# Attention and a token-mixing MLP on one core: exponentials over a bank pair, and ScalarE's side work ordered by deadlines

## The chip, the core and the metric

The kernel runs on one core of one Trainium2 chip. A core has TensorE (matmuls, shown in the profile as PE, its weight loads as PEld), VectorE (DVE), ScalarE (ACT), GpSimd (POOL) and SyncE (SP), which here only issues DMAs. Each engine works through its own instructions in order and waits for others at semaphores. Matmuls write to PSUM, eight banks of 512 fp32 columns on each of 128 partitions. The metric is the device time of one execution in microseconds (us).

## What is computed

`x` has 2048 tokens of 640 channels. The output mixes an attention block and a token-mixing MLP by a gate; all of it is fp32.

```
g = sigmoid((x * gate_w).sum(-1))
# A: 32 heads of 20
q, k, v = split(x @ wqkv)
p = softmax(q @ k.T * 20**-0.5)
a = concat(p @ v) @ wo
# B: MLP over the token axis, shared by the channels
h = layernorm(x)                       # over the 640 channels
u = gelu(einsum("sd,sf->df", h, w1) + b1)   # f = 1728
b = (u @ w2 + b2).T
out = g * a + (1 - g) * b
```

## The kernel before

Precision is kept by splitting each fp32 operand into a high part and a remainder (`hi_lo`, line 38): ScalarE copies the high part, and VectorE or GpSimd subtracts it from the source. A product is then three matmuls (high by high, high by low, low by high).

The program is one stream of Python calls. Engines whose order is "manual" (`manual_schedule`) keep the order in which the code emits their instructions: TensorE always, ScalarE and VectorE from the first unit on, GpSimd and SP from the MLP's preparation on. Where an instruction stands in the emission is therefore where it stands in its engine's queue.

The stages, in order of time:

- **Projections.** `qk_unit(m, w, q)` makes 128 rows of q or k for 512 tokens: 15 matmuls into one of four PSUM banks (`st_tile`, tags st0 to st3), then ScalarE copies the high part (`evh`), VectorE makes the remainder (`evl`), and SP stores both. For three row blocks of k it also makes differences of neighbouring blocks (`kf`, `dh`). `load_w` fetches a weight block by a DMA on ScalarE's queue and splits it. After 16 units come 32 units for v, whose weights are `wv`, loaded raw as `wvr` by SP and split by `split_wv`; then 24 more q and k units.
- **MLP, with the first half of the row maxima beside it.** `mlp` is a generator; each step is a pair of matmuls on the two row halves of the array (`pair64`), which run at the same time. It goes through two halves of the channels (`d`); in each, 14 tiles of u and 16 tiles of y. A tile uses two `st` banks. At its end ScalarE evacuates both (`u_evac`: `xg` and `x2`; `y_evac`: `ty` and `x2`), GpSimd adds them; for u follow the gelu and a split into `gh` and `gl`, for y the store to `y_d`. The weights come 512 columns at a time: SP loads `wr` (8 buffers), `w_split` makes `wh` on ScalarE and `wl` on GpSimd, and `w_need(k)` keeps splits four pieces ahead.
- Between MLP steps, `s_next` gives matmuls of a second stream: scores of queries by keys, of which only the row maximum is wanted, so that the exponentials can be shifted. They go in pairs over four banks (s twice, s3, pv). Of eight such matmuls, three (`s_over`) are read by ScalarE (`relu`, line 212, into `ov`), three (`s_two`) by VectorE together with an `ov`, two (`s_one`, line 203) by VectorE alone. 1082 of the 2050 positions of this stream are given beside the MLP.
- **The loop.** 16 pairs of heads, 32 iterations each: 512 iterations. An iteration has four score matmuls with keys on the partitions (`st_op`, line 787), each read by one exponential of 512 columns on ScalarE (line 789), two `s_next` while they last, and the four products p by v of the iteration before (`pv_flush`, line 743), which accumulate in the bank pv. The four scores go round five banks: st0 to st3 and s3.
- **The output.** Normalisation, the product with `wo` (lines 843 to 847) and the mix.

In the MLP, ScalarE's and GpSimd's later steps are held back by a count of MLP steps, and emitted in the loop over steps by `settle`:

```
soon.append([2, relu])                  # s_over: two steps after its matmul
soon.append([6, lambda: ...tensor_add(xg, xg, x2)])
soon.append([18 if f == f_order[-1] else 30, lambda: u_gelu(...)])
while len(w_got) < min(k + 4, len(w_list)):
    w_split(len(w_got))                 # in w_need: at once
```

Of the kernel before, what the change touches and what calls it, by code (L numbers as in the profile page):

```python
# [13 lines left out]
P = 128  # L14
# [16 lines left out]
def gated_mix(ctx, tc, xT, x, wqk, wv0, wv1, wo, w1, w1t, b1, w2, b2, out):  # L31
# [37 lines left out]
    psum = ctx.enter_context(tc.tile_pool(name="psum", bufs=1, space=PSUM))  # L69

    def st_tile(shape, name):
        n = st_count[0] % 4
        st_count[0] += 1
        return psum.tile(shape, F32, tag=f"st{n}", bufs=1, name=name)
# [131 lines left out]
    def s_over(p, half, t, j, kc, over):  # L206
        def f():
            ps = s_mm(p, half, t, j, kc)

            def relu():  # L210
                over[j, kc] = s_pool[0].tile([P, 512], F32, tag="over", bufs=3, name=f"ov{p}_{half}_{t}_{j}_{kc}")
                nc.scalar.activation(over[j, kc], ps, AF.Relu)  # L212
# [81 lines left out]
    def qk_unit(m, w, q):  # L294
# [23 lines left out]
        dh = p1.tile([P, 512], F32R, tag="evh", bufs=2, name=f"dh{c}_{q}")  # L318
# [21 lines left out]
    raws = [w_dma(0), w_dma(NC)]  # L340
    w = {0: load_w(0, raws[0])}
    load_x(0)
    w[NC] = load_w(NC, raws[1])
# [116 lines left out]
    w_raws, w_got = [], []  # L460
# [13 lines left out]
    def w_split(k):  # L474
        src, tail = w_list[k]
        raw = w_raws[k]
        n, m = src.shape[1], src.shape[2]
        if k < AHEAD:
            o = 8 * (k % 2)
            hi, lo = w_tmp[k // 2][:, o: o + 4], w_tmp[k // 2][:, o + 4: o + 8]  # L480
        else:
            hi = gp.tile([P, 4, P], F32R, tag="wh", bufs=5, name=f"wh{k}")
            lo = None if tail else gp.tile([P, 4, P], F32R, tag="wl", bufs=5, name=f"wl{k}")
        if tail:
            hi_lo(hi[:, :n, :m], hi[:, :n, m:], raw[:, :n, :m], hi_eng=nc.scalar, lo_eng=nc.gpsimd)
        else:
            hi_lo(hi[:, :n], lo[:, :n], raw[:, :n], hi_eng=nc.scalar, lo_eng=nc.gpsimd)
        w_got.append((hi, lo))
# [9 lines left out]
    hs = []  # L498
    for n, (m, q) in enumerate(units):
# [4 lines left out]
        if 3 <= n < NT + 3:  # L504
            hs.append(h_split(0, n - 3))
# [26 lines left out]
    soon = []  # L532

    def settle(all_=False):
        for e in soon:
            e[0] -= 1
        due = [e for e in soon if all_ or e[0] <= 0]
        for e in due:
            soon.remove(e)
            e[1]()  # L540

    def u_evac(f, d, ps, gh, gl):
        xg = gp.tile([P, HALF], F32, tag="xg", bufs=3, name=f"xg{d}_{f}")
        nc.scalar.activation(xg, ps[0], AF.Copy)
        x2 = half_sum(ps[1], 1.0)
        soon.append([6, lambda: nc.gpsimd.tensor_add(xg, xg, x2)])
        if f == FF:
            soon.append([7, lambda: u_swap(d, xg)])
            soon.append([70, lambda: nc.gpsimd.tensor_add(xg, xg, sws.pop())])
            soon.append([100, lambda: u_tail(f, d, xg, gh)])  # L550
        else:
            soon.append([18 if f == f_order[-1] else 30, lambda: u_gelu(f, xg, gh, gl)])
# [5 lines left out]

    sws = []

    def u_gelu(f, xg, gh, gl):
        nc.scalar.activation(xg, xg, AF.Gelu_apprx_tanh, bias=b1_t[:, f:f + 1])
        hi_lo(gh, gl, xg, hi_eng=nc.scalar, lo_eng=nc.gpsimd)
# [7 lines left out]
    def u_tail(f, d, xg, gh):  # L571
        nc.scalar.activation(xg, xg, AF.Gelu_apprx_tanh, bias=b1_t[:, f:f + 1])
        ht = gp.tile([P, HALF], F32R, tag="ht", bufs=1, name=f"ht{d}")
        nc.gpsimd.tensor_copy(ht[TL:], xg[TL:])
        nc.gpsimd.tensor_copy(gh[:TL], xg[:TL])
        nc.gpsimd.tensor_sub(gh[TL:], xg[TL:], ht[TL:].bitcast(F32))

    def y_evac(t, d, ps):
        ty = hp.tile([P, HALF], F32, tag="ty", bufs=3, name=f"ty{d}_{t}")
        c = slice(t, t + 1)  # L580
        nc.scalar.activation(ty, ps[0], AF.Identity, bias=b2o[:, c], scale=omg[:, c])
        x2 = half_sum(ps[1], omg[:, c])

        def rest():
            nc.gpsimd.tensor_add(ty, ty, x2)

        def store():
            (nc.sync if d and t == NT - 1 else nc.scalar).dma_start(y_d[t * P:(t + 1) * P, d * HALF:(d + 1) * HALF], ty)

        soon.append([6, rest])  # L590
        soon.append([24, store])

    def mlp(hs):
        k = 0
        for d in range(2):
            g = {}
            for f in f_order:
# [3 lines left out]
                ps = [st_tile([P, HALF], f"u{d}_{f}_{i}") for i in range(2)]  # L601
                for c in range(4):
                    wh, wl = w_need(k)
                    k += 1
                    for i in range(4):
                        hh, hl = hs[4 * c + i]
# [6 lines left out]
                u_evac(f, d, ps, gh, gl)  # L613
                g[f] = (gh, gl)
            for t in range(NT):
                ps = [st_tile([P, HALF], f"y{d}_{t}_{i}") for i in range(2)]
                for c in range(4):
                    wh, wl = w_need(k)
                    k += 1
                    for i in range(4 if c < 3 else 2):  # L620
                        f = 4 * c + i
                        gh, gl = g[f]
# [9 lines left out]
                if d and t == NT - 2:  # L632
                    nc.scalar.activation(eps_t, eps_t, AF.Exp)
                if d == 0:
                    if t == 0:
                        h_norm(1, 0)
                    if t + 1 < NT:
                        h_norm(1, t + 1)
                    hs[t] = h_split(1, t)
                    if t + 3 < NT:  # L640
                        h_load(1, t + 3)
# [11 lines left out]
    for n, _ in enumerate(steps):  # L653
        settle()
# [13 lines left out]
    settle(True)  # L668
# [23 lines left out]
    s_wide[0] = False  # L692
    s_src[NDIFF + 1] = s_stack(NDIFF + 1)
# [85 lines left out]
    def st_op(i):  # L779
        g, n = divmod(i, 4)  # L780
# [3 lines left out]
        j, c = 1 - n % 2, n // 2  # L784
        r = slice(64 * j, 64 * j + 3 * DH + 2)
        ps = psum.tile([P, 512], F32, tag="s3" if i % 5 == 4 else f"st{i % 5}", bufs=1, name=f"st{p}_{it}_{j}{c}")
        nc.tensor.matmul(ps, ks[r, kt * P:(kt + 1) * P], qs[qh][r, c * 512:(c + 1) * 512], start=True, stop=True)  # L787
        pt = lp.tile([P, 512], F32, tag="pt", bufs=12, name=f"p{p}_{it}_{j}{c}")
        nc.scalar.activation(pt, ps, AF.Exp, scale=SCALE)  # L789
        pts.setdefault(g, {})[j, c] = pt  # L790

    st_op(0)
    LEFT = NP * 128 + 2 - S_AHEAD
    for p in range(NP):
# [3 lines left out]
        for it in range(32):  # L798
# [34 lines left out]
    lps.close()  # L833

# [74 lines left out]
```

## Time and profile before

| | us |
|---|---|
| median of 3 runs (1860.96 to 1864.75) | 1861.8 |
| profiled execution, its own time | 1860.5 |
| its span in the profile | 1858.7 |
| projections (first qk matmul to last) | 7.3 to 229.0 |
| MLP with row maxima | 229.3 to 768.9 |
| loop (first exponential to the end of the last) | 770.8 to 1774.5 |
| output | 1775.5 to 1858.7 |

The profiled execution is the one that all rows below are from; it is 1.3 us under the median of the runs. In the rows, a group is "line engine operation, output<-input xcount | busy us, mean ns of one | idle us just before, and what ended it". Busy time counts overlapping instructions once, so a mean of one may be longer than busy time divided by the count: instructions of one engine overlap their start with the end of the one ahead. The table of windows gives, for each stretch, each engine's busy us and in brackets its instructions. A matmul's end is modelled, so TensorE reads as busy even where it has small gaps; its weight loads show those better.

### The profile page before, as it was taken

Reading aid. Unit: us, or ns where it says so; the run is one execution under the profiler, and the core shown is the slowest. Engines: PE = TensorE matmul, PEld = TensorE weight load, DVE = VectorE, ACT = ScalarE, POOL = GpSimd, SP = SyncE. Lnnn points to the kernel's source line nnn. Section 1 sums busy time; section 2 is a strip of 40 time slices with the busy share of each in tenths; the row PEclk is TensorE's granted clock in tenths of the full one; section 3 lists DMA queues with packets and bytes.
Section 4 is the critical chain, followed back from the end, with each engine's and each line's share of the span. In section 5 each row is a group of like instructions: output and inputs, shape, how many; then the busy total and the mean of one; then the engine's idle time right before and its main releaser. Section 6 shows DMA issues by size and latency. Waiting matters only on the chain. (4 is left out here: it accounts for less than half of the span.)

```text
span 1858.7 us, 39442 instructions
## 1 busy us (share of the span) xinstructions
PE 1829.8 (98%) x14978; PEld 1188.1 (64%) x14978; DVE 1239.4 (67%) x2407; ACT 1511.7 (81%) x3047; POOL 640.8 (34%) x898
## 2 busy tenths in 40 slices
PE   9899999999999999999999999999999999999998
PEld 7798799999999999644444444444444444444378
DVE  5303288888888888866666666666766667667137
ACT  4244378877788777599999999999999999999920
POOL 2112367778777777201111211121322121212210
PEclk9999999999999999999999999999999999999999
DMA  8646876556665555225222232042262322201463
GB/s 301 203 152 234 260 184 171 145 158 191 179 179 145 145 155 165 68 55 134 57 48 59 60 85 56 22 109 59 54 124 63 76 62 56 71 14 23 129 217 131
DMA packets 155662, 222.93 MB, mean 120 GB/s; under 512 B 65998, under 2 KB 92382, under 8 KB 152046
## 3 DMA queue, kind: packets, MB, share of 16 engines
q1 hardware_dynamic: 131008, 181.70, 35.8%
q0 software_dynamic: 15104, 23.01, 5.3%
q10 hardware_dynamic: 9360, 15.70, 2.5%
q8 instruction: 118, 1.93, 0.4%
q14 instruction: 72, 0.59, 0.1%
HBM read 165.43 MB, written 54.54 MB: 118 GB/s over the span
## 5 line engine op out<-in xcount | busy, mean ns | idle before, releaser
L203 DVE TENSOR_REDUCE mx<-s 128x1 f32<-128x512 f32 x1280 | 833.1, 686 | 303.0 <-PE s L197 296.6
L789 ACT ACTIVATE p<-st 128x512 f32<-128x512 f32 x2048 | 1003.6, 940 | 0.6 <-PE st L787 0.6
L787 PEld LDWEIGHTS st<-qs_True,ks_True 62*128 62x128 f32 x2048 | 336.0, 185 | 462.6 <-ACT p L789 434.7
L743 PE MATMUL pv<-p,v 128*32 128x512 f32 x4096 | 546.6, 605 | 0.2 <-PE st L787 0.2
L787 PE MATMUL st<-qs_True,ks_True 62*128 62x512 f32 x2048 | 529.3, 437 | 1.1 <-ACT x L556 1.1
L197 PE MATMUL s<-ks_False,qs_False 60*128 60x512 f32 x1152 | 315.2, 407 | 9.7 <-ACT ov L212 8.4
L197 PE MATMUL s<-sk,sq 60*128 60x512 f32 x896 | 324.0, 444 | 0.0
L43 POOL TENSOR_TENSOR wl<-wr,wh 128x512 fp32r<-128x512 f32 x228 | 276.3, 1217 | 107.9 <-ACT wh L40 70.9
L221 DVE CUSTOM_DVE_ANT_0 ov<-s,ov 128x512 f32<-128x512 f32 x384 | 263.6, 687 | 57.5 <-PE s L197 51.3
L212 ACT ACTIVATE ov<-s 128x512 f32<-128x512 f32 x384 | 224.7, 598 | 80.2 <-PE s L197 77.8
L730 POOL DMA_DIRECT2D o_d<-oev x128 | 66.8, 522 | 622.1 <-DVE oev L724 619.5
L48 PE MATMUL y<-gh,wh 64*128 64x320 f32 x896 | 196.7, 307 | 0.0
L48 PE MATMUL y<-gl,wh 64*128 64x320 f32 x832 | 188.3, 307 | 0.0
L48 PE MATMUL y<-gh,wl 64*128 64x320 f32 x832 | 186.5, 306 | 0.0
L40 ACT ACTIVATE wh<-wr 128x512 fp32r<-128x512 f32 (+2 forms) x246 | 147.6, 601 | 46.3 <-DMA wr<-in_wqk_dram 30.7
L197 PEld LDWEIGHTS s<-ks_False,qs_False 60*128 60x128 f32 x1152 | 164.6, 185 | 24.0 <-ACT ov L212 15.4
L743 PEld LDWEIGHTS pv<-p,v 128*32 128x32 f32 x4096 | 81.2, 108 | 125.1 <-issue 115.6
L48 PE MATMUL u<-hl,wh 64*128 64x320 f32 x864 | 161.0, 307 | 0.0
L48 PE MATMUL u<-hh,wh 64*128 64x320 f32 x864 | 160.7, 307 | 0.0
L48 PE MATMUL u<-hh,wl 64*128 64x320 f32 x800 | 149.9, 307 | 0.0
L48 PEld LDWEIGHTS y<-gh,wh 64*128 64x128 f32 x896 | 137.8, 185 | 1.2
L197 PEld LDWEIGHTS s<-sk,sq 60*128 60x128 f32 x896 | 130.7, 184 | 0.0
(129 smaller groups left out, 2108.2 us busy)
## 6 DMA issues: line engine op xcount, KB each, us to landing
wr<-in_w_dram SPq DMA_DIRECT2D x192, 256.0 KB
ks_True<-k_d SPq DMA_DIRECT2D x96, 160.0 KB
qs_True<-q_d SPq DMA_DIRECT2D x192, 80.0 KB
qs_False<-q_d SPq DMA_DIRECT2D x108, 80.0 KB
sk<-k_d SPq DMA_DIRECT2D x42, 160.0 KB
sq<-q_d SPq DMA_DIRECT2D x84, 80.0 KB
v_d<-vt SPq DMA_DIRECT2D x32, 168.0 KB
v<-v_d SPq DMA_DIRECT2D x16, 336.0 KB
```

The costliest lines, as they stand in the source:

```text
L40: nc.scalar.activation(hi, src, AF.Copy)
L43: (lo_eng or nc.vector).tensor_sub(lo, src, hi.bitcast(F32))
L48: nc.tensor.matmul(ps[k], a[r], b[r], start=start, stop=stop)
L197: nc.tensor.matmul(ps, qs[half][r, t * P:(t + 1) * P], ks[r, kc * 512:(kc + 1) * 512], start=True, stop=True)
L203: nc.vector.tensor_reduce(mx[:, slot, j, t: t + 1], ps, axis=AX.X, op=OP.max)
L212: nc.scalar.activation(over[j, kc], ps, AF.Relu)
L221: nc.vector.tensor_tensor_reduce(ov, ps, ov, 1.0, -3.0e38, OP.add, OP.max, mx[:, slot, j, t: t + 1])
L730: nc.gpsimd.dma_start(o_d[DH * h: DH * h + DH, cols], ev[r: r + DH, :])
L743: nc.tensor.matmul(pv[r: r + 32, :], v_tiles[p][:, kt, 10 * j: 10 * j + 32], pt[j, c], start=(kt == 0), stop=(kt == NT - 1))
L787: nc.tensor.matmul(ps, ks[r, kt * P:(kt + 1) * P], qs[qh][r, c * 512:(c + 1) * 512], start=True, stop=True)
L789: nc.scalar.activation(pt, ps, AF.Exp, scale=SCALE)
```

## The change

There are four edits.

**1. The loop's exponentials.** `st_op` is replaced by `st_pair` and `st_one`. In each iteration the two scores of the first 512 queries (heads j = 0 and 1) go to the two banks of one tile `two`, and one exponential of 1024 columns reads both. The other two scores go to single banks (one0, one1 and s3 in turn), each with an exponential of 512 columns. The pair has one buffer: 2 + 2 + 1 + 2 (s) + 1 (pv) are all eight banks. To make room, the four `st` banks get a pool of their own, closed before the loop (`four`), and one is opened again for the output (`late`). The order of TensorE's work changes: pair, one, two maxima, one, products. The score that was given one ahead of the loop is no longer there.

**2. ScalarE's order beside the MLP.** `settle` now takes nanoseconds: a clock advances by 146 for an MLP step and by 233 for a pair of maxima. ScalarE's work is put into a list with a cost, a delay before it may start and a slack (`act`), and whenever ScalarE is free by that clock, the entry that is allowed and has the earliest deadline is emitted. `force` emits from the lists until a condition holds, where something is needed at once. The two evacuations of a tile are separate entries; weight splits, five pieces ahead instead of four, have deadlines too; other steps go into a list of events by time. The stores of y move from ScalarE's queue to SP's.

**3. Loads of weights for the first projections.** The DMAs for the third and fourth weight blocks are issued one or several units earlier, and `wv` is split one unit earlier and ahead of the unit.

**4. The tile `dh`** of the first two k blocks has a buffer of its own instead of one of the two of `evh`.

```
-            soon.append([2, relu])
+            act(relu, 480, 350, 900)
...
+            force(lambda: (j, kc - 1) in over)
...
-        dh = p1.tile([P, 512], F32R, tag="evh", bufs=2, name=f"dh{c}_{q}")
+        if c == 2:
+            dh = p1.tile([P, 512], F32R, tag="evh", bufs=2, name=f"dh{c}_{q}")
+        else:
+            dh = (pvp if c else px).tile([P, 512], F32R, tag="dh", bufs=1, name=f"dh{c}_{q}")
...
+        if q == 1:
+            raws[1] = w_dma(1)
         if q == 2:
-            w[1] = load_w(1)
+            w[1] = load_w(1, raws[1])
+            raws[NC + 1] = w_dma(NC + 1)
...
+        if 2 <= n < 2 + NC:
+            split_wv(0, n - 2)
+            load_wv(1, n - 2)
         qk_unit((1, NC + 1)[n // 4], w[(1, NC + 1)[n // 4]], n % 4)
         if n == 0:
-            w[NC + 1] = load_w(NC + 1)
-        if n >= 3:
-            split_wv(0, n - 3)
-            load_wv(1, n - 3)
+            w[NC + 1] = load_w(NC + 1, raws[NC + 1])
...
     def w_need(k):
         while len(w_raws) < min(k + 9, len(w_list)):
             w_raw(len(w_raws))
-        while len(w_got) < min(k + 4, len(w_list)):
-            w_split(len(w_got))
-        return w_got[k]
+        while w_asked[0] < min(k + 5, len(w_list)):
+            j = w_asked[0]
+            act(lambda: w_split(j), 520, 0, 2200 * (j - k) - 4000)
+            w_asked[0] += 1
+        force(lambda: k in w_got)
+        return w_got.pop(k)
...
+    def act(fn, cost, delay, slack):
+        act_q.append((clock[0] + delay + slack, clock[0] + delay, next(count), cost, fn))
+
+    def act_emit(e):
+        act_q.remove(e)
+        free[0] = max(free[0], e[1]) + e[3]
+        e[4]()
+
+    def settle(ns):
+        clock[0] += ns
+        for e in sorted(e for e in events if e[0] <= clock[0]):
+            events.remove(e)
+            e[2]()
+        while free[0] <= clock[0] + 100:
+            e = min((e for e in act_q if e[1] <= clock[0] + 100), default=None)
+            if e is None:
+                break
+            act_emit(e)
...
+    def both(first, ps, scale, cost, then):
+        got = []
+        def second():
+            got.append(half_sum(ps[1], scale))
+            later_on(600, lambda: then(got[0]))
+        act(first, cost, 350, 3000)
+        act(second, cost - 80, 350, 3500)
...
-            (nc.sync if d and t == NT - 1 else nc.scalar).dma_start(y_d[...], ty)
+            later_on(4000, lambda: nc.sync.dma_start(y_d[...], ty))
...
-    def st_op(i):
-        j, c = 1 - n % 2, n // 2
-        ps = psum.tile([P, 512], F32, tag="s3" if i % 5 == 4 else f"st{i % 5}", bufs=1, ...)
-        nc.tensor.matmul(ps, ks[r, ...], qs[qh][r, ...], start=True, stop=True)
-        pt = lp.tile([P, 512], F32, tag="pt", bufs=12, ...)
-        nc.scalar.activation(pt, ps, AF.Exp, scale=SCALE)
+    def st_pair(g):
+        ps = tp.tile([P, 2, 512], F32, tag="two", bufs=1, name=f"st{g}_0")
+        for j in range(2):
+            st_mm(g, j, 0, ps[:, j])
+        pt = lp.tile([P, 2, 512], F32, tag="pp", bufs=3, name=f"p{g}_0")
+        nc.scalar.activation(pt, ps, AF.Exp, scale=SCALE)
+
+    def st_one(g, j):
+        n = (2 * g + j) % 3
+        ps = (psum if n == 2 else tp).tile([P, 512], F32, tag=("one0", "one1", "s3")[n], bufs=1, ...)
+        st_mm(g, j, 1, ps)
+        pt = lp.tile([P, 512], F32, tag="pt", bufs=6, name=f"p{g}_1{j}")
+        nc.scalar.activation(pt, ps, AF.Exp, scale=SCALE)
...
-            for n in range(4):
-                i = 4 * (p * 32 + it) + n + 1
-                if i < NP * 128:
-                    st_op(i)
-                if n < take:
-                    s_next()
+            st_pair(g)
+            st_one(g, 0)
+            for _ in range(take):
+                s_next()
+            st_one(g, 1)
```

What this does to the queues is shown at three places, as the built programs have them. A name like p9_12_11 is the exponential of head pair 9, iteration 12, j = 1, c = 1; in the changed program p300_0 is iteration 300's pair and p300_10, p300_11 its singles.

**TensorE in the loop**, one iteration, before:

```order
L787 MATMUL st9_12_00_22115<-qs9_True_0_21012,ks9_True_21011 128x512
L197 MATMUL s13_0_2_1_0_22119<-sk13_20327,sq13_0_20328 128x512
L787 MATMUL st9_12_11_22122<-qs9_True_0_21012,ks9_True_21011 128x512
L197 MATMUL s13_0_2_0_0_22126<-sk13_20327,sq13_0_20328 128x512
L787 MATMUL st9_12_01_22129<-qs9_True_0_21012,ks9_True_21011 128x512
L787 MATMUL st9_13_10_22133<-qs9_True_0_21012,ks9_True_21011 128x512
L743 MATMUL pv9_0_21746<-p9_11_00_22089,v9_21198 32x512
L743 MATMUL pv9_0_21746<-p9_11_01_22103,v9_21198 32x512
L743 MATMUL pv9_0_21746<-p9_11_10_22076,v9_21198 32x512
L743 MATMUL pv9_0_21746<-p9_11_11_22096,v9_21198 32x512
```

and in the changed program:

```order
L861 MATMUL st334_0_22098<-qs10_True_0_21046,ks10_True_21045 128x512 x2
L861 MATMUL st334_10_22103<-qs10_True_0_21046,ks10_True_21045 128x512
L199 MATMUL s13_1_2_1_2_22107<-sk13_19616,sq13_1_19618 128x512
L199 MATMUL s13_1_2_0_2_22110<-sk13_19616,sq13_1_19618 128x512
L861 MATMUL st334_11_22113<-qs10_True_0_21046,ks10_True_21045 128x512
L820 MATMUL pv10_0_21725<-p333_0_22078,v10_21216 32x512
```

The same ten matmuls in three neighbouring pairs on opposite row halves and four products; the two of the pair now stand first and together, and write one tile. ScalarE's queue in the loop, before and in the changed program:

```order
L789 ACTIVATE p9_12_00_22117<-st9_12_00_22115 128x512
L789 ACTIVATE p9_12_11_22124<-st9_12_11_22122 128x512
L789 ACTIVATE p9_12_01_22131<-st9_12_01_22129 128x512
L789 ACTIVATE p9_13_10_22135<-st9_13_10_22133 128x512
```

```order
L868 ACTIVATE p300_0_21221<-st300_0_21218 128x1024
L876 ACTIVATE p300_10_21225<-st300_10_21223 128x512
L876 ACTIVATE p300_11_21235<-st300_11_21233 128x512
L868 ACTIVATE p301_0_21245<-st301_0_21242 128x1024
```

Four exponentials an iteration have become three, over the same columns.

**ScalarE beside the MLP**, at the end of the first tile of y. `ty` and `x` are the two evacuations, `hh` the split of the next half's normalised input, `wh` a weight split, `ov` a maximum's read. Before:

```order
L212 ACTIVATE ov_0_4_1_0_5181<-s_0_4_1_0_5172 128x512
L40 ACTIVATE wh_5185<-wr_4914 128x512
L581 ACTIVATE ty_0_5204<-y_0_0_5024,b2o,omg 128x320
L556 ACTIVATE x_5206<-y_0_1_5025,omg 128x320
L40 ACTIVATE hh_0_5210<-xm_0_4798 128x320
L40 ACTIVATE wh_5220<-wr_4971 128x256
L212 ACTIVATE ov_0_4_1_2_5226<-s_0_4_1_2_5196 128x512
L212 ACTIVATE ov_0_4_0_0_5245<-s_0_4_0_0_5238 128x512
```

and in the changed program:

```order
L214 ACTIVATE ov_0_4_1_0_5186<-s_0_4_1_0_5179 128x512
L40 ACTIVATE wh_5196<-wr_4980 128x256
L214 ACTIVATE ov_0_4_1_2_5211<-s_0_4_1_2_5203 128x512
L655 ACTIVATE ty_0_5213<-y_0_0_5028,b2o,omg 128x320
L214 ACTIVATE ov_0_4_0_0_5236<-s_0_4_0_0_5232 128x512
L584 ACTIVATE x_5244<-y_0_1_5029,omg 128x320
L40 ACTIVATE wh_5257<-wr_5030 128x512
L40 ACTIVATE hh_0_5270<-xm_0_4802 128x320
```

The read ov_0_4_1_2 stood behind `ty`, `x`, `hh` and a `wh`; it stands ahead of the first three now, and the next `ov` stands between the two evacuations.

**ScalarE in the first projections**, around the split of the fourth weight block (wh_505 before, wh_508 now). Before:

```order
L40 ACTIVATE evh_3_433<-qk_3_417 128x512
L40 ACTIVATE dh_3_442<-kf_2_393 128x512
L40 ACTIVATE evh_0_497<-qk_0_481 128x512
L281 DMA wr_503<-in_wqk_dram 128x640
L40 ACTIVATE wh_505<-wr_503 128x640
L40 ACTIVATE evh_1_525<-qk_1_509 128x512
```

and in the changed program, from the DMA on:

```order
L284 DMA wr_352<-in_wqk_dram 128x640
L40 ACTIVATE evh_2_370<-qk_2_354 128x512
L40 ACTIVATE evh_2_392<-qk_2_376 128x512
L40 ACTIVATE evh_3_416<-qk_3_400 128x512
L40 ACTIVATE evh_3_438<-qk_3_422 128x512
L40 ACTIVATE dh_3_447<-kf_2_398 128x512
L40 ACTIVATE evh_0_502<-qk_0_486 128x512
L40 ACTIVATE wh_508<-wr_352 128x640
```

The DMA now stands seven instructions ahead of the split that needs it, instead of right before it. SP's queue is ordered freely in this part; there the five loads of `wvr` stood right after the stores of the fourth unit, and stand after those of the ninth now.

More of the change, by code (lines that the diff above doesn't have):

```diff
@@ L69, in gated_mix @@
     psum = ctx.enter_context(tc.tile_pool(name="psum", bufs=1, space=PSUM))
+    four = ExitStack()
+    banks = [four.enter_context(tc.tile_pool(name="four", bufs=1, space=PSUM))]
     def st_tile(shape, name):
@@ L531, in gated_mix, with later_on, force @@
     s_pool[0] = hp
[L532 to L552, printed above, removed]
+    clock, free, count = [0], [0], iter(range(10 ** 6))
+    act_q, events = [], []
+    def act(fn, cost, delay, slack):
+        act_q.append((clock[0] + delay + slack, clock[0] + delay, next(count), cost, fn))
+    def later_on(delay, fn):
+        events.append((clock[0] + delay, next(count), fn))
+    def act_emit(e):
[12 more added lines that the diff above has]
+            act_emit(e)
+    def force(cond):
+        while not cond():
+            if act_q and (not events or min(act_q)[0] <= min(events)[0]):
+                act_emit(min(act_q))
+            else:
+                e = min(events)
+                events.remove(e)
+                e[2]()
+    evacs = []
     def half_sum(ps, scale):
@@ L667, in gated_mix @@
             done += 2
-    settle(True)
+            settle(233)
+    force(lambda: not act_q and not events)
     while done < S_AHEAD:
@@ L692, in gated_mix @@
     s_wide[0] = False
+    four.close()
+    trio = ExitStack()
+    tp = trio.enter_context(tc.tile_pool(name="trio", bufs=1, space=PSUM))
     s_src[NDIFF + 1] = s_stack(NDIFF + 1)
@@ L833, in gated_mix @@
     lps.close()
+    trio.close()
+    banks[0] = ctx.enter_context(tc.tile_pool(name="late", bufs=1, space=PSUM))
     ep = ctx.enter_context(tc.tile_pool(name="ep", bufs=1, side="right"))
```

99 lines of the change are left out of this document (63 added, 36 removed).

## The prediction

> **What bounds the kernel now.** I read the page's busy rows first, then a table of windows by stage, then, stage by stage, the waits of TensorE's weight loads and the timeline at single stalls.
>
> ```profile
> PE 1829.8 (98%) x14978; PEld 1188.1 (64%) x14978; DVE 1239.4 (67%) x2407; ACT 1511.7 (81%) x3047; POOL 640.8 (34%) x898
> ...
> 771.00:1774.00 1003.00, 1002.83 (x7104) 416.93 (x7100) 655.75 (x1058) 1003.00 (x2048) 186.17 (x363) 1.00 0.30 68
> 229.00:364.00 135.00, 133.33 (x1586) 129.52 (x1586) 112.85 (x285) 105.99 (x211) 99.52 (x103) 0.99 0.62 166
> 364.00:500.00 136.00, 130.98 (x1566) 125.85 (x1564) 119.72 (x296) 107.28 (x214) 104.06 (x112) 1.00 0.62 174
> ...
> 634.00:769.00 135.00, 133.92 (x1567) 125.34 (x1563) 120.78 (x281) 90.08 (x175) 88.28 (x94) 1.00 0.43 126
> 7.20:68.30 61.10, 57.88 (x240) 45.88 (x241) 31.71 (x51) 24.48 (x45) 8.80 (x19) 0.97 0.88 294
> 68.30:145.10 76.80, 73.14 (x481) 72.34 (x481) 9.39 (x29) 29.51 (x70) 12.31 (x44) 0.98 0.49 159
> 145.20:229.00 83.80, 83.80 (x362) 67.88 (x360) 24.59 (x39) 31.71 (x58) 27.80 (x36) 1.00 0.78 251
> ```
>
> The page's 98% for TensorE is an average over stages with different limits. In the loop (first window) ScalarE is busy for every one of 1003.00 us, so it sets the pace; TensorE reads as busy too, but its weight loads wait there. In the MLP (the next three) ScalarE has a fifth to a third of its time free and TensorE should run through; what it loses are single stalls. Of the projections, the last window runs clean: 83.8 us for 360 matmuls, 0.233 us each. The two ahead of it don't.
>
> **The loop's exponentials.** The rows of one iteration, and the groups for their price:
>
> ```profile
> L789 ACT ACTIVATE p<-st 128x512 f32<-128x512 f32 x2048 | 1003.6, 940 | 0.6 <-PE st L787 0.6
> ...
> PEld st L787 <- ACT p L789: 434.7, 539, 0.8
> ...
> 1299.19 5.84 ACT L789 ACTIVATE p<-st 128x512 f32<-128x512 f32 x11
> ...
> 1301.61 0.18 PEld L787 LDWEIGHTS st<-qs_True,ks_True 62*128 62x128 f32 x1 [0.84 <-ACT p L789]
> 1301.61 0.49 PE L787 MATMUL st<-qs_True,ks_True 62*128 62x512 f32 x1
> ...
> 1301.95 0.69 PE L787 MATMUL st<-qs_True,ks_True 62*128 62x512 f32 x3
> 1302.17 1.29 DVE L203 TENSOR_REDUCE mx<-s 128x1 f32<-128x512 f32 x2 [0.67 <-PE s L197]
> ...
> 1302.57 1.07 PE L743 MATMUL pv<-p,v 128*32 128x512 f32 x8
> 1303.57 0.18 PEld L787 LDWEIGHTS st<-qs_True,ks_True 62*128 62x128 f32 x1 [0.84 <-ACT p L789]
> ...
> L743 PE MATMUL pv<-p,v 128*32 128x512 f32 x4096 | 546.6, 605 | 0.2 <-PE st L787 0.2
> ...
> L40 ACT ACTIVATE ohe<-ore 128x1024 fp32r<-128x1024 f32 x6 | 6.4, 1061 | 33.9 <-PE a L843 33.9
> ...
> L40 ACT ACTIVATE ohl<-orl 128x512 fp32r<-128x512 f32 x4 | 2.5, 629 | 7.8 <-DVE orl L766 7.8
> ```
>
> 1003.6 us for 2048 exponentials are 0.490 us each, though one lasts 0.940: they overlap, and eleven take 5.84 = 0.94 + 10 x 0.49. An iteration is four, 1.96 us, as the two weight loads at 1301.61 and 1303.57 show. No row has an exponential of 1024 columns. The nearest are copies on ScalarE: 1061 ns for 1024 columns, 629 for 512, so 512 more columns cost 432 ns. An exponential of 0.490 is then 0.432 of columns and 0.058 that is paid per instruction; a wide one costs 0.922 where two cost 0.980. An iteration comes to 1.902, and 512 of them save 512 x 0.058 = 30 us. The bounds: nothing, if the 0.058 is paid per bank and not per instruction, and 33 us, if a column costs 1.5% less than the copies' 0.844 ns.
>
> The Trainium skill, "ScalarE: Activation LUTs" (What ACT_TABLE_LOAD costs), states 186 ns + 0.833 ns a column, with back-to-back instructions overlapping by some 93; that makes 520 for 512 columns, where the trace has 490, and would save 93 x 512 = 48 us. By it the total below would be 18 us lower; the measured 490 decides against it.
>
> Does TensorE keep up? Its own work in an iteration starts at 1301.61; the products start at 1302.57 and last 1.07 with a mean of 0.605 for one, so the second round of four starts 0.46 after the first, and both are through by about 1303.49. That is at most 1.88 of 1.96, of which some 0.10 is a weight load laid bare by the wait (the first score takes 0.49, the next ones start 0.34 later where two matmuls in a row cost 0.233). So 1.902 leaves 0.02 to 0.1 us: ScalarE stays the bound, barely.
>
> The pair has one buffer, so its two matmuls can start only when its exponential is over. They take 0.49, and a reader starts 0.07 after a matmul's end (1301.61 + 0.49 to VectorE's 1302.17). ScalarE meanwhile has the two single exponentials, 0.98. So 0.56 stands under a cover of 0.98. The lead was five banks, 2.45 us; with about 0.4 left, waits that were hidden may show. The nearest row is the wait for the bank pv, once in 16 iterations, when VectorE copies it out: 7.5 us in 31 waits, 0.24 each, under 0.4.
>
> ```profile
> PEld pv L743 <- DVE oev L724: 7.5, 31, 0.2
> ```
>
> I charge it nothing. Behind a late score everything on TensorE waits in order, so if that cover goes, it costs its excess 31 times, a few us. The loop no longer starts with a score made ahead: the first exponential waits for 0.56, +0.6 us once. The last score, products and output keep their order.
>
> **ScalarE's order beside the MLP.**
>
> ```profile
> PEld s L197 <- ACT ov L212: 15.4, 27, 1.5
> PEld s L197 <- DVE mx L203: 7.2, 25, 0.7
> ...
> 372.56 0.62 ACT L581 ACTIVATE ty<-y,b2o,omg 128x320 f32<-128x320 f32 x1 [0.26 <-PE y L48]
> 373.08 0.52 ACT L556 ACTIVATE x<-y,omg 128x320 f32<-128x320 f32 x1
> 373.94 0.47 ACT L40 ACTIVATE hh<-xm 128x320 fp32r<-128x320 f32 x1 [0.34 <-DVE xm L440]
> 374.32 0.40 ACT L40 ACTIVATE wh<-wr 128x256 fp32r<-128x256 f32 x1
> 374.63 1.06 ACT L212 ACTIVATE ov<-s 128x512 f32<-128x512 f32 x2
> ...
> 375.26 0.50 PE L197 MATMUL s<-ks_False,qs_False 60*128 60x512 f32 x2 [1.19 <-ACT ov L212]
> ```
>
> The first two rows are the weight loads' waits from 229 to 769; the others are the longest of them. Its place is the one whose order is shown above: `ov` stood behind `ty`, `x`, `hh` and `wh`, 2.07 us from 372.56 on with 0.34 for VectorE in it, and the next matmul into that bank stood still for 1.2 us. With the changed order this read stands ahead of `ty`, `x` and `hh`. All 27 waits are of this kind, so 15.4 us is what the reordering can take away. It can't take the 7.2 that end with VectorE, and VectorE is nearly full: 119.72 of 136 us and 120.78 of 135. When TensorE gains 8 us in such a stretch, VectorE's share goes from 88 to 94%, and part of the gain comes back as waits for `mx`. The other bound is a loss: if the new order makes gelus or weight splits late (GpSimd is at 104.06 of 136, and the splits now come with a slack), I price it by the row of waits for VectorE doubled, +7. I take 10 of the 15.4 as gained, nearer to the row that the edit aims at. The y stores on SP's queue cost ScalarE less and SP 32 more issues; weights are asked for eight pieces ahead there, so a store that waits for GpSimd is covered; nothing.
>
> **The first projections.**
>
> ```profile
> PEld qk L54 <- ACT wh L40: 3.0, 1, 3.0
> PEld v L54 <- DVE wv L43: 2.4, 2, 1.9
> PEld v L54 <- ACT wv L40: 2.0, 1, 2.0
> ...
> 55.04 0.63 PE L54 MATMUL qk<-xl,wh 128*128 128x512 f32 x1
> 55.46 0.63 PE L54 MATMUL qk<-xh,wl 128*128 128x512 f32 x1
> ...
> 68.35 0.46 PE L54 MATMUL v<-wv,xh 128*128 128x322 f32 x2
> ...
> 69.69 0.31 PE L54 MATMUL v<-wv,xh 128*128 128x322 f32 x1
> ```
>
> 240 matmuls at 0.233 are 55.9 us and took 61.1; 480 for v at 0.149 (nine from 68.35 to 69.69) are 71.5 and took 76.8. Of these 10.5 us lost, 7.4 are waits for weight splits that came late, and after each stall matmuls start 0.42 apart instead of 0.233 for some us (55.04 to 55.46). About 2 lie at the very start and stay. With the DMA seven instructions ahead of its split and `wv` one unit earlier I take 7 of the remaining 8.5. Against it: the `wvr` loads now stand five units later on SP's queue, and DMA is at 0.88 of its time in the first window. If they come late, one of the waits for `wv` returns (-3 instead of -7). `dh` out of the `evh` buffers costs nothing on the path.
>
> **The sum**, against the profiled execution's 1860.5: -30 (loop) + 0.6 (its start) - 10 (MLP) - 7 (projections) = 1814. The median of the runs is 1.3 above that execution, so 1815.
>
> **Rivals.**
>
> *TensorE becomes the loop's bound.* If two weight loads per iteration are laid bare (one after the pair's release, one where the fourth product waits for the last single exponential, which ends 0.98 after the pair's, just when TensorE gets there at 0.96), its 1.88 grows to about 1.94. The loop then saves 512 x 0.02 = 10 us, and the time is 1835. For it: the margin of 0.02. Against it: a late TensorE doesn't wait at the release, and gets that 0.10 back. Chance 0.11.
>
> *The wide exponential costs two narrow ones.* Loop unchanged, 1845. Against it: the copies' 1061 against 629. Chance 0.06.
>
> *The fixed share is larger* (93 ns): 1797. Chance 0.03.
>
> *TensorE's clock falls in the loop, and the change loses.* Place: TensorE now stops at the pair's release in each iteration. Matmuls at 0.42 instead of 0.233 would make its 1.8 us about 3.2, 1.3 over the forecast's iteration; the gain of 47 us is gone when 36 of the 512 iterations run so, and a tenth of them would give 1882. Against it: the loop before has such a stop too (0.84 in the weight loads' row, 539 times) with a granted clock of 1.00, and only stops of 2 to 3 us lowered it. The Trainium skill, "TensorE: Matmul & The Clock Gate" (A second HAM failure mode: psum-queue depth-cycling), tells of a kernel whose cycling through PSUM banks made TensorE pause often enough for its clock to swing; by that rule this could happen here, and the 1.00 of the loop does not agree with it. Chance 0.04.
>
> **How the numbers follow.** The forecast has 0.76. Its own range takes the loop from -24 to -33, the MLP from -15 to +7, the projections from -10 to -2: all low is 1803, all high is unlikely together, 1832. With the first rival the range for 8 in 10 is 1798 to 1836; it leaves out the others. A measurement of this kernel tells about 0.2% (3.7 us) from no change; all cases but the last are beyond that on the fast side: faster 0.94, same 0.02, slower 0.04.
>
> **What would show it.** Loop: the wide group near 0.92 us apart from its successor, ScalarE still busy all the time, iteration 1.90; wrong if ScalarE shows waits for scores or iterations of 1.94 and more. MLP: the waits of weight loads for `ov` down from 15.4 to a few us, those for `mx` up; wrong if waits for `wl`, `gh` or `gl` appear. Projections: no wait for `wh` near 50 us, first v matmul before 66. The prediction fails most likely in the loop's lead: a wait on VectorE or a DMA of more than 0.4 us that five banks had hidden.

## The result: 1815.8 us, forecast 1815

| | us |
|---|---|
| changed kernel, median of 4 runs (1813.47 to 1816.69) | 1815.77 |
| kernel before, 4 runs beside it (1860.96 to 1864.75) | 1863.24 |
| ratio, 95% interval | 0.9744 [0.9727, 0.9761] |
| profiled execution of the changed kernel, its span | 1813.47, 1811.7 |

The time is the one forecast, but two of its terms were off, in opposite directions. By stage, from the two traces:

| us | before | after | difference | forecast |
|---|---|---|---|---|
| projections | 7.3 to 229.0 | 7.2 to 218.1 | -10.8 | -7 |
| MLP with maxima (first u matmul to last y) | 229.3 to 768.9 | 218.5 to 753.4 | -4.6 | -10 |
| loop (first to last exponential) | 770.8 to 1774.5 | 755.4 to 1729.9 | -29.1 | -29.4 |
| output | 1775.5 to 1858.7 | 1731.0 to 1811.7 | -2.5 | 0 |

The page's busy row, then the table of windows by stage of the changed kernel (columns as for before: each engine's busy us and instructions, the granted clock, the DMA share):

```profile
PE 1787.1 (99%) x14978; PEld 1109.4 (61%) x14978; DVE 1239.9 (68%) x2407; ACT 1484.3 (82%) x2535; POOL 642.5 (35%) x898
...
7.20:63.00 55.80, 55.36 (x241) 44.94 (x241) 32.71 (x53) 24.59 (x45) 8.87 (x19) 1.00 0.94 320
63.00:134.30 71.30, 71.10 (x481) 70.83 (x480) 8.31 (x27) 27.18 (x65) 12.29 (x44) 1.00 0.53 170
134.40:218.40 84.00, 84.00 (x361) 67.83 (x360) 23.83 (x38) 31.82 (x61) 27.71 (x35) 1.00 0.77 244
218.50:360.10 141.60, 131.62 (x1584) 131.09 (x1585) 113.35 (x286) 109.18 (x214) 100.77 (x104) 0.96 0.61 166
360.10:490.80 130.70, 129.63 (x1568) 126.69 (x1566) 120.69 (x297) 107.60 (x214) 104.78 (x112) 1.00 0.62 175
490.80:620.60 129.80, 129.79 (x1592) 129.48 (x1590) 113.27 (x287) 107.92 (x214) 102.35 (x107) 1.00 0.65 173
620.60:753.40 132.80, 132.24 (x1564) 126.14 (x1561) 120.37 (x279) 90.84 (x174) 87.97 (x94) 1.00 0.44 130
756.00:1729.00 973.00, 972.29 (x7099) 337.63 (x7099) 655.65 (x1058) 971.21 (x1535) 185.79 (x362) 1.00 0.31 71
```

Three MLP windows shrank from 134 to 136 us to 130 to 133; the first one grew to 141.6 with TensorE idle for ten of them. In the loop ScalarE is still busy throughout (971.21 of 973). TensorE's 972.29 tells nothing of its load, since it read as full before too (1002.83 of 1003.00). The loop's groups on ScalarE, and one iteration from the timeline:

```profile
L876 ACT ACTIVATE p<-st 128x512 f32<-128x512 f32 x1024 | 570.7, 631 | 0.0
L868 ACT ACTIVATE p<-st 128x1024 f32<-128x1024 f32 x512 | 540.0, 1055 | 2.5 <-PE st L861 1.9
...
1301.34 1.08 ACT L876 ACTIVATE p<-st 128x512 f32<-128x512 f32 x2
1301.71 0.29 PEld L861 LDWEIGHTS st<-qs_True,ks_True 62*128 62x128 f32 x3 [0.84 <-ACT p L868]
1301.72 0.73 PE L861 MATMUL st<-qs_True,ks_True 62*128 62x512 f32 x3
...
1302.06 0.62 PE L199 MATMUL s<-sk,sq 60*128 60x512 f32 x2
...
1302.29 0.40 PE L861 MATMUL st<-qs_True,ks_True 62*128 62x512 f32 x1
1302.32 1.03 ACT L868 ACTIVATE p<-st 128x1024 f32<-128x1024 f32 x1
...
1302.62 1.07 PE L820 MATMUL pv<-p,v 128*32 128x512 f32 x8
1303.24 1.08 ACT L876 ACTIVATE p<-st 128x512 f32<-128x512 f32 x2
1303.61 0.29 PEld L861 LDWEIGHTS st<-qs_True,ks_True 62*128 62x128 f32 x3 [0.84 <-ACT p L868]
```

From 1302.32 the wide exponential runs for 0.92 until the next one starts at 1303.24, and from 1301.34 the two narrow ones take 0.98 together: 1.90 an iteration on ScalarE. TensorE's round from 1301.72 to 1303.61 is 1.89. ScalarE sets the pace, and e4 below tells how little TensorE has to spare. Waits of weight loads at the MLP's start (218 to 232), then in the rest of it (232 to 754):

```profile
PEld s L199 <- ACT ov L214: 10.3, 1, 10.3
...
PEld s L199 <- DVE mx L205: 6.7, 24, 0.4
PEld s L199 <- DVE mx L224: 2.1, 5, 0.6
```

The 27 waits for `ov`, 15.4 us before, are gone, and one new wait of 10.3 us is there. Its place, on TensorE and on ScalarE after the change, and then on ScalarE before:

```profile
220.67 0.39 PE L199 MATMUL s<-ks_False,qs_False 60*128 60x512 f32 x1
231.04 0.79 PE L199 MATMUL s<-ks_False,qs_False 60*128 60x512 f32 x1 [9.98 <-ACT ov L214]
...
229.88 0.63 ACT L40 ACTIVATE wh<-wr 128x512 fp32r<-128x512 f32 x1 [6.71 <-DMA k_d<-evl]
230.41 1.07 ACT L214 ACTIVATE ov<-s 128x512 f32<-128x512 f32 x2
```

```profile
232.12 1.78 ACT L212 ACTIVATE ov<-s 128x512 f32<-128x512 f32 x3 [0.32 <-PE s L197]
237.83 0.63 ACT L40 ACTIVATE wh<-wr 128x512 fp32r<-128x512 f32 x1 [3.92 <-DMA k_d<-evl]
```

The order of ScalarE's queue there, in the changed kernel:

```
L40 ACTIVATE wh_2193<-wr_2151 128x512
L214 ACTIVATE ov_0_0_1_0_2202<-s_0_0_1_0_2198 128x512
L214 ACTIVATE ov_0_0_1_2_2217<-s_0_0_1_2_2210 128x512
```

and before:

```
L212 ACTIVATE ov_0_0_1_0_2197<-s_0_0_1_0_2191 128x512
L212 ACTIVATE ov_0_0_1_2_2212<-s_0_0_1_2_2203 128x512
L212 ACTIVATE ov_0_0_0_0_2229<-s_0_0_0_0_2223 128x512
L40 ACTIVATE wh_2233<-wr_2148 128x512
```

This first `wh` of the MLP goes into space that the projections' buffers held, and may not start until their last store (`k_d<-evl`) has landed. Before, the three reads ahead of it were done by 233.9, and TensorE's waits for `ov` in the first 12 us came to 1.6 us. Now the split waits until 229.88, the reads wait behind it in order, and TensorE stands at the first score whose bank is not read. During the stop and behind it the granted clock is lower (0.62 from 224 to 228, 0.50 to 232 and 0.60 to 236), which makes 0.96 over the window from 218.5 to 360.1.

### The profile page after: what moved, and what is told of

Its sections match the earlier page's. It is cut to its first block, busy times and chain, and to the rows that moved or that the text cites. A ratio compares the mean times of both kernels' runs of the same rounds, so it can differ in the third digit from the quotient of the medians.

```text
span 1811.7 us, 39932 instructions
## 1 busy us (share of the span) xinstructions
PE 1787.1 (99%) x14978; PEld 1109.4 (61%) x14978; DVE 1239.9 (68%) x2407; ACT 1484.3 (82%) x2535; POOL 642.5 (35%) x898
## 3 DMA queue, kind: packets, MB, share of 16 engines
q8 instruction: 118, 1.93, 0.4%
## 5 line engine op out<-in xcount | busy, mean ns | idle before, releaser
L876 ACT ACTIVATE p<-st 128x512 f32<-128x512 f32 x1024 | 570.7, 631 | 0.0
L868 ACT ACTIVATE p<-st 128x1024 f32<-128x1024 f32 x512 | 540.0, 1055 | 2.5 <-PE st L861 1.9
L861 PEld LDWEIGHTS st<-qs_True,ks_True 62*128 62x128 f32 x2048 | 246.7, 185 | 436.2 <-ACT p L868 427.3
L199 PE MATMUL s<-ks_False,qs_False 60*128 60x512 f32 x1152 | 393.8, 399 | 11.6 <-ACT ov L214 10.0
L199 PE MATMUL s<-sk,sq 60*128 60x512 f32 x896 | 280.3, 394 | 0.0
L48 PE MATMUL u<-hl,wh 64*128 64x320 f32 x864 | 226.4, 307 | 0.0
L48 PE MATMUL u<-hh,wh 64*128 64x320 f32 x864 | 226.3, 307 | 0.0
L199 PEld LDWEIGHTS s<-ks_False,qs_False 60*128 60x128 f32 x1152 | 211.2, 185 | 21.9 <-ACT ov L214 10.3
L48 PE MATMUL u<-hh,wl 64*128 64x320 f32 x800 | 214.0, 307 | 0.0
L199 PEld LDWEIGHTS s<-sk,sq 60*128 60x128 f32 x896 | 166.0, 186 | 17.9
```

Source lines behind the costliest of these rows:

```text
L48: nc.tensor.matmul(ps[k], a[r], b[r], start=start, stop=stop)
L199: nc.tensor.matmul(ps, qs[half][r, t * P:(t + 1) * P], ks[r, kc * 512:(kc + 1) * 512], start=True, stop=True)
```

## Experiments

The runs were made on three chips, each with the kernel before beside it on the same chip (medians 1866.92, 1865.80 and 1865.93), so only differences and ratios against that one are compared.

### One edit at a time

**e1**: the kernel before with the loop's edit alone (`st_pair`, `st_one`, the pools, the order in the iteration).

> Only the loop's edit (pair tile, three exponentials an iteration, the PSUM pools). Theory (the wide exponential saves one instruction's fixed share, 0.06 us an iteration): iteration 1.90 instead of 1.96, loop 974 us instead of 1004, total 29 to 32 us under before, some 1832; if the output's 2.5 us come with it, 1830. Rival (part of the loop's gain comes from the other edits): loop 985 or more, total over 1842.

1836.55, 0.9838 [0.9823, 0.9852]: -30.4 us. The table of windows for its loop reads as in the whole change:

```profile
778.00:1752.00 974.00, 973.12 (x7104) 339.73 (x7104) 655.92 (x1058) 972.08 (x1536) 185.53 (x363) 1.00 0.32 70
```

**e2**: the kernel before with the MLP's edit alone (`act`, `settle`, `force`, `both`, the y stores on SP).

> Only ScalarE's order beside the MLP, with the y stores on SP. Theory (the order takes away nearly all waits for ov, some 15 us, and gives part back in one wait at the MLP's start, where the first weight split now stands ahead of the first ov reads and waits for a DMA): stretch from first u matmul to last y matmul 531 to 533 us instead of 539.5, waits for ov outside its first 12 us under 2 us, one wait of 6 to 8 us in them; total 6 to 9 us under before, some 1855. Rival (the wait at the start comes only with the faster projections): no such wait here, stretch 525, total 1847.

1858.39, 0.9960 [0.9946, 0.9974]: -8.5 us. Its waits, from the MLP's start and then from 243 on:

```profile
PEld s L197 <- ACT ov L212: 10.2, 1, 10.2
...
PEld s L197 <- DVE mx L203: 6.7, 24, 0.4
PEld s L197 <- ACT ov L212: 4.0, 2, 2.5
PEld s L197 <- DVE mx L222: 2.2, 5, 0.6
```

The long wait is there with the old projections too, so it comes from the new order and not from projections that end earlier. The MLP took 538.8 us, where two kernels with the old order on the same chip (e1 and e3) took 544.4 and 543.5. The total came as expected, the parts did not: 531 to 533 us, a wait of 6 to 8 us at the start and under 2 us of later waits for `ov` were expected, and it was 538.8, 10.2 and 4.0.

**e3**: the kernel before with the projections' edits alone (loads earlier, `split_wv` one unit earlier, `dh`).

> Only the earlier weight loads and splits and dh's own buffer. Theory: the last projection matmul ends near 218 instead of 229, the rest is unchanged, total 9 to 11 us under before, some 1852. Rival (the MLP's start waits for the last stores of k, which DMA lands no earlier): the MLP's first 12 us grow by 3 to 5 us, total 1856 to 1858.

1856.76, 0.9944 [0.9927, 0.9961]: -10.2 us. The projections end at 220.3 (231.0 in e1, with the old projections on the same chip). At the MLP's start the wait is 3.8 us (3.9 in e1), later the old ones stand:

```profile
PEld s L197 <- ACT ov L212: 15.3, 26, 1.6
```

The MLP did not grow (543.5 us, 544.4 in e1), so what the projections gain is not given back there. The three differences add up to -49.1; the whole change gave -47.5, and -48.2 when it was run again (c1).

### The new wait

**e5**: the changed kernel, with no weight split allowed before 8 us of the MLP's clock.

```
-            act(lambda: w_split(j), 520, 0, 2200 * (j - k) - 4000)
+            act(lambda: w_split(j), 520, max(0, 8000 - clock[0]), 2200 * (j - k) - 4000)
```

> The changed kernel, with weight splits of the MLP held back for its first 8 us, so that the first ov reads stand ahead of the first split in ScalarE's queue. Theory (the 10.3 us wait at the MLP's start is that order): TensorE goes on for some 8 to 9 us and then waits only for the split itself, whose inputs land 11 us after the start; wait 3 to 5 us instead of 10.3, total 5 to 7 us under the changed kernel, some 1809. Rival (the wait is the DMA's, whatever the order): the same wait under another name, total 1814 to 1816.

1812.29, 0.9706 [0.9691, 0.9721]. The MLP takes 529.6 us (534.9 in the changed kernel); the waits from 215 to 769:

```profile
PEld s L199 <- ACT ov L214: 3.9, 2, 3.6
...
PEld u L48 <- POOL wl L43: 0.6, 1, 0.6
```

**c1** (the changed kernel) and **c2** (e5) were run again, each on one of the other two chips:

> The changed kernel once more, to stand on one chip beside the others here: 2.4 to 2.7% under before. The wait at the MLP's start again 8 to 11 us (theory: it is an order, and shows in each run); rival (it was a DMA that happened to be late): under 4 us.

> The version with splits held back for the MLP's first 8 us, again, beside the two others on one chip: 2.8 to 3.1% under before, wait at the start 3 to 5 us. Rival (its gain over the changed kernel was a difference between chips): 2.4 to 2.7% under before.

c1 gave 0.9742 [0.9725, 0.9759] with a wait of 10.8 us at the start, c2 0.9702 [0.9677, 0.9726] with 4.2. Against its own kernel before, e5 is 54.6 and 53.4 us faster, the changed kernel 47.5 and 48.2: putting this one split behind the first reads is worth 5 to 7 us. The two never ran on one chip; e9 below, which has the split in its old place, is 7.4 us slower than c2 on the same chip.

**e8**: the changed kernel with weight splits emitted at once, four pieces ahead, as before; all else by deadlines.

```
-        while w_asked[0] < min(k + 5, len(w_list)):
-            j = w_asked[0]
-            act(lambda: w_split(j), 520, 0, 2200 * (j - k) - 4000)
+        while w_asked[0] < min(k + 4, len(w_list)):
+            w_split(w_asked[0])
             w_asked[0] += 1
-        force(lambda: k in w_got)
```

> The changed kernel, but the MLP's weight splits are emitted as before: at once where the piece is asked for, four ahead; the reads ov, the evacuations and the rest keep their deadlines. Theory (the wait at the start is the split's place ahead of the first ov reads; the waits for ov later on come from bursts of which the splits are only a part): start 2 to 5 us of wait instead of 10, waits for ov later on 2 to 6 us instead of 0 to 1.4; total 3 to 6 us under the changed kernel. Rival (the splits at once were the whole of the old waits): waits for ov later on 12 us and more, total 4 to 8 us over it.

1811.89, 0.9706 [0.9676, 0.9737], an MLP of 529.3 us. Its waits for `ov` in the MLP:

```profile
PEld s L199 <- ACT ov L214: 6.0, 6, 4.0
```

Of the 6.0 us, 5.1 lie between 219 and 243 us, so the later waits are 0.9, less than the 2 to 6 expected. e8 and e5 are alike: the splits' deadlines bring nothing that these runs show. As the y stores bring nothing either (e9), the gain is put down to the rest of the edit, the deadlines of the reads and evacuations; that part was not run alone.

**e9**: the changed kernel with the y stores back on ScalarE's queue.

```
-            later_on(4000, lambda: nc.sync.dma_start(y_d[...], ty))
+            later_on(4000, lambda: (nc.sync if d and t == NT - 1 else nc.scalar).dma_start(y_d[...], ty))
```

> The changed kernel with the y stores back on ScalarE's queue, at the places that the new order gives them. Theory (an issue takes 0.33 us of the sequencer, beside the running instruction): 0 to 3 us over the changed kernel, waits for ov in the y stretches 0 to 3 us. Rival (the stores in ScalarE's queue were a good part of the old waits): 5 us and more over it.

1819.97, 0.9741 [0.9717, 0.9765]: no difference to c1's 0.9742 is seen. Costing that part at nothing was right.

### What bounds the loop now

**e6**: the changed kernel, the pair read by two exponentials of 512 columns; tile, banks and order stay.

```
-        nc.scalar.activation(pt, ps, AF.Exp, scale=SCALE)
+        for j in range(2):
+            nc.scalar.activation(pt[:, j], ps[:, j], AF.Exp, scale=SCALE)
```

> The changed kernel, but the pair's tile is read by two exponentials of 512 columns, all else as it is. Theory (the gain is one instruction's fixed share): iteration 1.96, loop 1003 us, total 28 to 31 us over the changed kernel. Rival (banks and order of TensorE's work made the gain): iteration 1.90, total as the changed kernel.

1848.15, 0.9906 [0.9891, 0.9922], 30.5 us over c1. The window of its loop:

```profile
757.00:1762.00 1005.00, 1004.19 (x7106) 418.80 (x7106) 656.75 (x1058) 1003.84 (x2048) 185.83 (x363) 1.00 0.31 68
```

The loop is back at 1.96 an iteration with ScalarE full. So the gain of the loop is the instruction that is no longer there; of the banks or the order no gain is seen.

**e4**: the changed kernel with both pairs of scores read by wide exponentials, each pair with a tile of its own.

```
-            st_pair(g)
-            st_one(g, 0)
+            st_pair(g, 0)
             for _ in range(take):
                 s_next()
-            st_one(g, 1)
+            st_pair(g, 1)
```

> The changed kernel with both pairs of scores read by an exponential of 1024 columns each (two tiles of two banks, one buffer each): pair, two maxima, pair, products. Theory (ScalarE's fixed share per instruction was what the loop gained; TensorE's own work is at most 1.88 us an iteration): ScalarE's bound falls to 1.83, TensorE becomes the bound at 1.85 to 1.88, loop 947 to 963 us against 974, total 12 to 27 us under the changed kernel. Rival (two releases an iteration lay two weight loads bare, each behind a wait): 1.92 to 1.96, loop 983 to 1003, total 10 to 30 us over it.

1874.96, 1.0045 [1.0031, 1.0059]: 0.45% slower than the kernel before, 57 us over c1. My theory failed; the rival had the direction, though the loss is larger than it said. The profile is of the fastest of six executions, 1868.83. The window, the group, and the timeline of two iterations on TensorE:

```profile
752.00:1783.00 1031.00, 1027.33 (x7105) 347.42 (x7106) 656.19 (x1058) 984.12 (x1024) 186.33 (x363) 1.00 0.30 67
L868 ACT ACTIVATE p<-st 128x1024 f32<-128x1024 f32 x1024 | 984.4, 1022 | 47.0 <-PE st L861 42.5
...
1290.00 0.50 PE L861 MATMUL st<-qs_True,ks_True 62*128 62x512 f32 x2
1290.34 0.39 PE L199 MATMUL s<-sk,sq 60*128 60x512 f32 x2
1290.69 0.51 PE L861 MATMUL st<-qs_True,ks_True 62*128 62x512 f32 x2
1291.13 1.07 PE L820 MATMUL pv<-p,v 128*32 128x512 f32 x8
1292.12 0.50 PE L861 MATMUL st<-qs_True,ks_True 62*128 62x512 f32 x2
1292.46 0.40 PE L199 MATMUL s<-sk,sq 60*128 60x512 f32 x2
1292.69 0.40 PE L861 MATMUL st<-qs_True,ks_True 62*128 62x512 f32 x2
1293.02 1.07 PE L820 MATMUL pv<-p,v 128*32 128x512 f32 x8
1294.02 0.50 PE L861 MATMUL st<-qs_True,ks_True 62*128 62x512 f32 x2
```

ScalarE waits for 47 us: it is no longer the bound alone. Here a long iteration, 2.12 us (1290.00 to 1292.12), is followed by one of 1.90; of the 473 full iterations in the middle of the loop, 210 took 1.88 to 1.93 and 237 took 2.04 to 2.16. In the longer one the second pair comes 0.35 after the maxima instead of 0.23, and the products 0.44 after it instead of 0.33. A timeline of the weight loads shows why, with the exponential that releases the pair in the last two rows:

```profile
1300.16 0.19 PEld L861 LDWEIGHTS st<-qs_True,ks_True 62*128 62x128 f32 x2 [0.84 <-ACT p L868]
1300.62 0.19 PEld L861 LDWEIGHTS st<-qs_True,ks_True 62*128 62x128 f32 x2 [0.16 <-ACT p L868]
...
1299.56 1.02 ACT L868 ACTIVATE p<-st 128x1024 f32<-128x1024 f32 x1
1300.79 2.89 ACT L868 ACTIVATE p<-st 128x1024 f32<-128x1024 f32 x3 [0.21 <-PE st L861]
```

The exponential from 1299.56 ends at 1300.58, and the second pair's weight load starts at 1300.62: it waited for that release, and could not be made ahead of its matmul. The load at 1300.16 has the same name behind it (0.84), but no exponential ends there: one runs from 1299.56 to 1300.58, and the one ahead of it had ended about 0.5 us before the load. So the idle time ahead of the first score, behind the products, is not a wait for ScalarE. It is 0.99 to 1.00 from the first product to the next score in both iterations here, in the changed kernel (1302.62 to 1303.61) and before (1302.57 to 1303.57). Over the middle of the loop the two loads differ throughout: the first pair's starts 0.23 to 0.53 us after its release, the second pair's always 0.05 after it. In the short iterations that is early enough: at 1292.59 the load is 0.10 ahead of its matmul, behind the maxima. Even these take 1.88 at the least and 1.90 here, though ScalarE would allow 1.84 (two of 0.92): that is TensorE's own floor. In the long ones TensorE waits for ScalarE, and then ScalarE for the late scores (0.21 ahead of 1300.79), so neither runs through.

**e7**: e4 with e5's edit.

> Two wide exponentials and the weight splits held back for the MLP's first 8 us. If both hold, their gains add: 18 to 34 us under the changed kernel, and 5 to 7 under the two wide exponentials alone.

1874.29, 1.0046 [1.0027, 1.0064]. The sum failed with e4, and the split's 5 to 7 us did not show either: the two medians are 0.7 us apart. In the profiles the MLP is 2.3 us shorter than in e4 (529.7 us; the wait at its start is 3.7 instead of 7.8) and the loop 4.6 longer. As e4's profile is 6 us under its median and e7's is not, that does not settle where the gain went.

## Why the forecast came out right, and where it was not

- **Loop, -30: right.** -29.1 in the trace and -30.4 alone (e1). The 0.058 per instruction, taken from two copies, measured 0.060 (two narrow 0.980, one wide 0.920, each the median from start to start), and e6 gives 30.5 / 512 = 0.060. So the rivals of a wide exponential that costs two narrow ones, and of a fixed share of 93 ns, are refuted. The Trainium skill, "ScalarE: Activation LUTs" (What ACT_TABLE_LOAD costs), gives 186 ns per instruction and an overlap of some 93; by an estimate from these, e6 would have been 512 x 93 ns = 48 us slower than c1. It was 30.5, so the measurement does not agree with it. The loop's start, +0.6, was mis-sized: the gap from the last y matmul to the first exponential grew by 0.1 us (1.9 to 2.0 by the table above).
- **"ScalarE stays the bound, barely": right, with one step wrong.** ScalarE has no idle time that counts (2.5 us in 974), and the rival at 1.94 with TensorE as the bound did not come true. The wrong step is what TensorE's "at most 1.88" is made of: the "0.10 laid bare by the wait" is no wait, since the load behind the products lies bare however early its bank is free (e4), and a TensorE that is late does not get it back. I had let the products end 0.92 after their start; the next score starts 0.99 after it. The scores took 0.90 instead of 0.96. The floor is 1.88 to 1.90, so the margin was at most 0.02 and not up to 0.1.
- **The pair's refill and the lead: right.** ScalarE's idle ahead of the wide exponential is 2.5 us in 512 iterations. The refill starts later than I had it, in the median 0.26 us after the release, because TensorE is still at its products. The waits for the bank pv grew, as said, from 7.5 to 11.3 us (31 waits, 0.36 each), without an effect that the loop's time shows.
- **Clock: the rival is refuted, and its premise did not hold.** The loop's clock stayed at 1.00. But in the changed kernel TensorE does not stop at the pair's release, as the 0.26 us above show; in e4 the second pair's load waits for its release in every iteration, and the clock of that loop is 1.00 too. The Trainium skill, "TensorE: Matmul & The Clock Gate" (A second HAM failure mode: psum-queue depth-cycling), tells of a kernel whose pauses between groups of matmuls, with PSUM banks cycled each iteration, let the clock swing; the 1.00 of both loops does not agree with it. That "only stops of 2 to 3 us lowered it" was read too narrowly: before, the clock was 0.69 from 236 to 240, behind waits of at most 1.4 us.
- **MLP, -10: too much, in the size of two parts.** -4.6 in the trace, -8.5 [-10.1, -4.9] alone (e2). Of the 15.4 us of waits all went, not 10; waits for VectorE rose from 7.2 to 8.8, as said. What I missed is a wait of 10.3 at the start. It is a loss of another kind than those I named (gelus or splits made late): a split made too early. I had compared the two orders at the end of the first y tile and not at the MLP's first instructions, where the order shows the split ahead of the first `ov`. -15.4 + 10.3 + 1.6 is -3.5 of the -4.6 in the trace; the rest I can't assign. One pair of traces is a weak measure here: with the new order and the split in its place of the changed kernel, the MLP took 532 to 539 us in six profiles, with the old order 539.6 to 544.4 in three.
- **Projections, -7: too little.** -10.8 and -10.2 alone (e3). Three sizes were off. The price of 0.233 for a matmul of the first window was too high: from 20 to 50 us, where nothing waits, they start 0.229 apart, so 240 are 54.9, the loss was 6.2 and not 5.2, and 5.3 of it went. Of the 2 us that I left at the very start, only 0.9 is in what is left of this window. And of the remaining 8.5 I had taken 7, where for v the window's whole loss of 5.3 went as well. The `wvr` loads five units later cost nothing: no wait for `wv` is left in the trace. The granted clock of the first two windows rose with it, from 0.97 and 0.98 to 1.00.
- **Output, 0: right.** The -2.5 is no effect of the change: the stretch took 80.7 to 84.7 us in the profiles of kernels that don't differ in it (83.0 in e1, 84.7 in e3, 82.5 in e5, 83.5 in c1).

The MLP's term, 5 too much by the trace, and the projections' term, 4 too little, cancelled. That the total is met within 1 us is luck; the loop's term is right by its working.

## What to carry to other kernels

A list that orders work by deadlines has to know of waits outside it: here the first instruction that reused a region of memory waited for the last store out of it (6.7 us), and in a queue that runs in order everything behind it waited too. Read the new order at each stage's first instructions, not only in its steady part. Where one engine "barely" stays the bound, work out the other engine's round from start to start in the trace, not from durations: here a second saving of the same kind made the kernel slower.

## What the runs showed of the hardware that I had not expected

- One exponential can read two PSUM banks without a price for the second bank: 0.920 us from start to start for 1024 columns, against 0.980 for two of 512 in the same loop. Worked out from copies of one tile it was 0.922.
- Behind products on 32 columns, the next score's weight load was hidden in no iteration of the loops before, after and in e4: it is at least 0.995 us from the first of eight products to the next score, where the products' own second round starts 0.45 after the first. In e4 the bank had been free for 0.23 us or more by then.
- A release that TensorE had to wait for ahead of the second pair of scores (e4) cost twice: in the iteration shown, 0.12 us for the late weight load and 0.11 more up to the products, 2.12 us instead of 1.90.
